# Attention and a gated MoE layer on one core: one pair's x transposed on TensorE, and the first MoE matmuls of three chunks in whole tiles

## The chip, the core and the metric

The kernel runs on one core of a Trainium2 chip. The metric is the device time of one execution in microseconds (us), a median over runs. The engines are named as in the profile: PE is TensorE (with PEld for its weight loads), ACT is ScalarE, DVE is VectorE, POOL is GpSimd, and SP is SyncE, which computes nothing here and only issues DMAs.

## The reference, cut to what matters

Batch B = 8, heads H = 8, tokens per batch S = 576, head size D = 64. Attention is causal with a window of 128 and a bias that falls with distance; its output, 4608 rows of 512, is the input x of a layer with 2048 hidden columns.

```python
scores = scale * np.matmul(q, k.transpose(0, 1, 3, 2))
bias = slopes[:, None, None] * (-np.abs(rel))[None, :, :]
mask = (rel >= 0) & (rel < window)
scores = np.where(mask, scores + bias[None], -1e9)
attn = softmax(scores)
out = np.matmul(attn, v)
x = out.transpose(0, 2, 1, 3).reshape(B * S, H * D)
h = x @ w_in
g = h * np.cos(h)
return g @ w_out
```

## The kernel before

**Units of attention.** A batch is split into nine units. Unit (pr, G) is head pair pr (0 to 3, two heads, 128 rows of x) and token group G: G = 0 is tokens 0 to 255 of the batch, G = 1 tokens 256 to 511. The ninth unit, the tail, is tokens 512 to 575 of all heads. A unit runs through PE (scores, L631, for the tail L621), ACT (exponential, L668), DVE (a multiplication with a stored bias mask, L686 to L693), PE (PV, the product with V, L725 and L728, for the tail L711 and L713), and DVE (division by the sum of the row, L765 and L767, into a buffer `xnat`). Units are run three at a time: (0,0), (1,0), (2,0); then (3,0), (0,1), (1,1); then (2,1), (3,1) and the tail. The three use PSUM bank pairs (2,3), (4,5), (6,7).

**x has to be transposed** into `xT` (head pair's 128 columns on the partitions, tokens along the free side) before it can enter the MoE layer. `x_back` does that, in one of two ways: batches 0 and 1 with two TensorE transposes into the unit's own PSUM bank (L800) and a copy by ACT or DVE (`flex`, L419 and L420); batches 2 to 7 with a DMA transpose that SP issues (L788; for the tail L780).

**MoE.** The 4608 tokens are cut into nine chunks of 512, which do not line up with batches of 576: chunk 2 is tokens 1024 to 1535, and batch 2 begins at token 1152. MoE1 makes h for a chunk: 16 column groups fc of 128, each a sum over the four head pairs kc. It has two forms. The whole form (`moe1`, L837) has four matmuls of 512 columns for one fc. The half form (`moe1_half`, L852) takes 256 tokens (hf = 0 or 1) and two column groups, and has eight matmuls of 256 columns. Either fills one PSUM bank of 512 columns, followed by a cosine on ACT (L823) and a multiplication on DVE (L829) into `gT`. MoE2 (L863) multiplies `gT` with w_out, 64 matmuls of 512 columns per chunk, copies the result to `ob` (L419, L420) and stores it by an SP DMA (L877).

**Rounds.** Round c does MoE1 of chunk c, and then attention of batch c + 1 with MoE2 of chunk c filling PE in between. Near its end MoE1 of chunk c + 1 begins as well. In chunks 1 to 3 all of MoE1 is in half form; in chunks 4 to 7 the first 8 of 16 column groups are in half form (all four fc pairs for hf 0, then for hf 1) and the other 8 whole; chunk 8 is whole. Chunk 0 has its own hand-written list.

What a chunk needs of the newest batch: chunk 2, hf 0 (tokens 1024 to 1279) reaches 128 tokens into batch 2, so it needs the G = 0 units of all four pairs; hf 1 (1280 to 1535) needs their G = 1 units too. Chunk 5 (2560 to 3071) reaches 192 tokens into batch 5, chunk 6 (3072 to 3583) 128 tokens into batch 6, chunk 7 (3584 to 4095) 64 tokens into batch 7; in each only hf 1 does.

**What sets the order.** Each operation is recorded with what it reads and writes, an estimated duration and a priority. A list scheduler (`Plan.schedule`) orders the operations of every engine but POOL, from estimates of its own, and `emit` writes one fixed sequence per engine with the semaphore waits that are needed. So each engine runs strictly in its written order, and an operation that waits holds up all behind it. DMA issues of SP stand in one queue: x transposes (L788, L780), the transposes of the next batch's q and k (L590) and the output stores (L877). POOL issues the loads of q, k (L454) and v (L463) in the order in which they are recorded; from batch 4 on they wait for an x transpose of an earlier batch.

Of the kernel before, what the change touches and what calls it, by code (L numbers as in the profile page):

```python
# [20 lines left out]
SPLIT = 4  # L21
# [89 lines left out]
class Plan:  # L111
# [16 lines left out]
    def op(self, eng, fn, r=(), w=(), dma=None, occ=100, lat=None, pri=5, mode=0, table=None,  # L128
           pk=None, after=(), behind=()):
        o = Op()  # L130
        o.seq = len(self.all)
        o.eng = (eng,) if isinstance(eng, str) else tuple(eng)
        o.fn, o.r, o.w, o.dma = fn, tuple(r), tuple(w), dma
        o.occ, o.lat, o.pri, o.mode, o.table = occ, occ if lat is None else lat, pri, mode, table
        o.pk, o.banks = pk, {k[1]: None for k in o.w if k[0] == "B"}
        preds = {d: ORDER for d in behind}
        preds.update((d, DATA) for d in after)
        for k in o.r:
            if k in self.writer:
                preds[self.writer[k]] = DATA  # L140
        for k in o.w:
            if k in self.writer:
                preds[self.writer[k]] = DATA
                if k[0] == "B":
                    o.banks[k[1]] = self.writer[k]
            for d in self.readers.get(k, ()):
                preds.setdefault(d, WAR)
        if dma is not None and dma in self.lastdma:
            preds[self.lastdma[dma]] = DATA
        if eng == "pool":  # L150
            if eng in self.lastseq:
                preds.setdefault(self.lastseq[eng], ORDER)
            self.lastseq[eng] = o
        if dma is not None:
            self.lastdma[dma] = o
        o.preds, o.succs, o.npred = preds, [], len(preds)
        for d in preds:
            d.succs.append(o)
        for k in o.r:
            self.readers.setdefault(k, []).append(o)  # L160
        for k in o.w:
            self.writer[k], self.readers[k] = o, []
        self.all.append(o)
        return o
# [199 lines left out]
def bass_alibi_sliding__then__act_gcu_kernel(  # L364
# [8 lines left out]
    with ExitStack() as ctx:  # L373
# [43 lines left out]
        def flex(o, i, w, n, pri, after=()):  # L417
            op(("act", "dve"),
               {"act": lambda e: e.activation(o, i, ACTF.Copy),  # L419
                "dve": lambda e: e.tensor_copy(o, i)},  # L420
               w=w, occ={"act": 95 + int(0.84 * n), "dve": 70 + int(1.05 * n)},
               lat={"act": 200 + int(0.84 * n), "dve": 140 + int(1.05 * n)}, pri=pri,
               after=after)
# [63 lines left out]
        def turn(kind):  # L487
            if phase[0] % 2 != kind:
                phase[0] += 1
                f = ACTF.Sin if kind else ACTF.Exp  # L490
                op("act", lambda e: e.activation(warm[:, :], halfpi[:, 0:1], f, scale=0.5),  # L491
                   r=["halfpi"], w=["warm"], occ=150, lat=230, table=phase[0], pri=0)
# [107 lines left out]
        def units(b):  # L600
            full = [(pr, G) for G in range(2) for pr in range(NPAIR)]
            return [(b, u) for u in full + [("t", None)]]
# [171 lines left out]
        def xkeys(pr, t0, n):  # L774
            return [("xT", pr, t // 64) for t in range(t0, t0 + n, 64)]

        def x_back(b, u, s, i):
            if u[0] == "t":
                t0 = S * b + 512
                o = op("sp", [lambda e: e.dma_start_transpose(xT[:, :, t0:t0 + 64], xtl[i][:, :])],  # L780
                   r=[("xtl", i)], w=[k_ for pr in range(NPAIR) for k_ in xkeys(pr, t0, 64)],
                   dma=f"xt{i}", occ=1250, pk=(256, 0.92, True), pri=2)
                xops.append(o)
                return
            pr, G = u
            t0 = S * b + 256 * G
            if b >= 2:
                o = op("sp", [lambda e: e.dma_start_transpose(  # L788
                    xT[:, pr, t0:t0 + 256].rearrange("p (r t) -> p r t", r=2), xnat[i][:, :])],
                   r=[("xnat", i)], w=xkeys(pr, t0, 256), dma=f"xb{i}", occ=1250,  # L790
                   pk=(256, 0.92, True), pri=2)
                xops.append(o)
                return
            bank = SLOT[s][0]
            dst = ps[:, bank, :].bitcast(BF16)[:, 768:1024]

            def f(e):
                ins = None
                for r in range(2):
                    ins = e.transpose(dst[:, 128 * r:128 * r + 128],  # L800
                                      xnat[i][:, 128 * r:128 * r + 128], ident[:, :])
                return ins
            op("pe", f, r=[("xnat", i), "ident"], w=[("B", bank)], occ=120, lat=290, pri=0)
            flex(xT[:, pr, t0:t0 + 256], dst, [("B", bank)] + xkeys(pr, t0, 256), 256, 0)
# [27 lines left out]
        def moe1(c, fc, bank):  # L832
            ci = ccount[0] % NCOS
            ccount[0] += 1
            gi = c % 2
            for kc in range(NPAIR):
                op("pe", lambda e, kc=kc: e.matmul(  # L837
                    ps[:, bank, :], w_in[:, kc, 128 * fc:128 * fc + 128],
                    xT[:, kc, CH * c:CH * c + CH], start=(kc == 0), stop=(kc == NPAIR - 1)),
                   r=xkeys(kc, CH * c, CH) + [("wi", fc)], w=[("B", bank)],  # L840
                   occ=216, lat=379, pri=5)
            gcu(c, bank, gT[gi][:, fc, :], [("g", gi, fc, 0), ("g", gi, fc, 1)], ci)

        def moe1_half(c, hf, f2, bank):
            ci = ccount[0] % NCOS
            ccount[0] += 1
            gi = c % 2
            t0 = CH * c + 256 * hf
            for i in range(2):
                fc = 2 * f2 + i  # L850
                for kc in range(NPAIR):
                    op("pe", lambda e, i=i, fc=fc, kc=kc: e.matmul(  # L852
                        ps[:, bank, 256 * i:256 * i + 256], w_in[:, kc, 128 * fc:128 * fc + 128],
                        xT[:, kc, t0:t0 + 256], start=(kc == 0), stop=(kc == NPAIR - 1)),
                       r=xkeys(kc, t0, 256) + [("wi", fc)], w=[("B", bank)],
                       occ=110, lat=271, pri=5)
            gcu(c, bank, gT[gi][:, 2 * f2:2 * f2 + 2, 256 * hf:256 * hf + 256],
                [("g", gi, 2 * f2 + i, hf) for i in range(2)], ci)
# [22 lines left out]
        def moe2(c):  # L881
            yield
            for t in range(4):
                cols = [(0, 512, OB[t % 2])] if c < NCH - 1 or t < 3 else [(0, 384, 1), (384, 128, 2)]
                for c0, wd, bank in cols:
                    moe2_mm(c, t, bank, c0, wd)
                    store(c, t, bank, c0, wd)
# [12 lines left out]
        def load_qk(b, after=()):  # L900
            for t in range(NBLK):
                load_nat("q", q, b, t, after)
                load_nat("k", k, b, t, after)
# [17 lines left out]
        for c in range(NCH):  # L921
            turn(1)
            if c:
                n = (0, 8, 8, 8, SPLIT, SPLIT, SPLIT, SPLIT, 0)[c]
                for i in range(2 * n):
                    moe1_half(c, i // n, i % n, 2 + i % 6)
                for i in range(16 - 2 * n):
                    moe1(c, 2 * n + i, 2 + (2 * n + i) % 6)
            second = moe2(c)
            if c + 1 < B:  # L930
                us = units(c + 1)
                if c == 0:
                    play(1, SECOND)
                else:
                    cross_transposes(c + 1)
                    if c == 1:
                        load_v(2, after=crossed[3:4])
                        load_qk(3)
                        load_v(3)
                    for g in range(0, 9, 3):  # L940
                        run(us[g:g + 3], (1, 2, 3))
            if c == 0:
                load_qk(2)
            else:
                if 3 < c + 2 < B:
                    load_v(c + 2, after=xops[3:4] if c > 2 else xops[-1:])
                if c + 3 < B:
                    load_qk(c + 3, xops[-1:])
            for _ in second:
                pass  # L950
# [29 lines left out]
```

## Time and profile before

| | us |
|---|---|
| median of 4 runs | 313.27 (312.67 to 314.71) |
| the profiled execution | 313.67 |
| its span in the profile | 311.6 |

The granted TensorE clock was 1.0 throughout. The groups around the change, from the table of the costliest groups (count, busy us, mean ns of one):

| group | count | busy | mean |
|---|---|---|---|
| L863 PE, MoE2, mostly 512 columns | 565 | 132.4 | 373 |
| L852 PE, MoE1 half form, 256 columns | 768 | 90.5 | 273 |
| L837 PE, MoE1 whole form, 512 columns | 186 | 41.5 | 379 |
| L800 PE, transposes of x | 32 | 4.5 | 221 |
| L419 ACT, copy of x after them, 128x256 | 8 | 3.0 | 380 |
| L823 ACT, cosine | 144 | 94.9 | 686 |
| L829 DVE, multiplication | 144 | 95.1 | 686 |
| L788 SP, x transposes by DMA | 48 | | 4.4 us to landing (2.3 to 8.6) |

A PE row's mean is the time of one matmul from start to its modelled end; matmuls overlap, so their pace is read from the chain of waits, which charges each only until the next one starts. Some records of matmuls are missing (565 of 576 for MoE2, 186 of 192 for the whole form). "Landing" is the time from a DMA's issue to its semaphore. The times in the views are from the span's start.

### The profile page before, as it was taken

What the parts mean: (1) busy time and instruction counts of PE and PEld (TensorE: products, weight loads), DVE (VectorE), ACT (ScalarE), POOL (GpSimd) and SP (SyncE); (2) the same over time, 40 slices, a digit from 0 to 9 for tenths busy, and PEclk for the clock granted to TensorE, in tenths of its full rate; (3) what the DMA queues carried; (4) which work ended last, traced back from release to release, by engine and by line L of the source; (5) the groups of instructions that cost most, each with busy time, mean ns of one, the idle gap of its engine ahead of it and who ended that gap; (6) DMA issues with size and microseconds to landing.
All of it is one profiled execution on the core that took longest, in us unless ns stands there. A gap on an engine that the chain in (4) does not pass through costs nothing.

```text
span 311.6 us, 6884 instructions
## 1 busy us (share of the span) xinstructions
PE 299.8 (96%) x2738; PEld 186.0 (60%) x2772; DVE 196.9 (63%) x445; ACT 204.6 (66%) x298; POOL 105.9 (34%) x134
## 2 busy tenths in 40 slices
PE   6799999999979999999999999999999999999996
PEld 4488555884558557855754485456645764444444
DVE  3898667786668767876787578755867684353000
ACT  8797846985567748874986488746784786462211
POOL 8999910049706400780356054605000000000000
PEclk9999999999999999999999999999999999999999
DMA  9999999969999982999999999999933300101112
GB/s 133 166 194 193 192 173 191 164 78 164 182 151 139 144 127 68 119 154 187 144 179 150 184 125 153 141 147 153 119 70 93 76 13 0 67 2 67 67 69 101
DMA packets 160895, 39.25 MB, mean 126 GB/s; under 512 B 148960, under 2 KB 156384, under 8 KB 160864
## 3 DMA queue, kind: packets, MB, share of 16 engines
q0 software_dynamic: 109552, 18.10, 80.3%
q1 hardware_dynamic: 51312, 20.72, 35.3%
q8 instruction: 22, 0.36, 0.5%
q14 instruction: 9, 0.07, 0.1%
HBM read 36.70 MB, written 9.44 MB: 148 GB/s over the span
## 4 chain that ended last, share of the span: by engine, by line
PE 82%; DMA 8%; POOL 7%; issue 2%; DVE 1%; ACT 0%; POOLq 0%
PE ps L863 37%; PE ps L852 22%; PE ps L837 13%; DMA vp<-in_v_dram 5%; PE ps L631 4%; DMA xT<-xnat 3%; PE ps L725 2%; POOL w_inb L470 2%; PE ps L728 1%; POOL vp L463 1%; POOL w_outb L477 1%; PE ps L711 1%; POOL qnat L427 1%; POOL knat L427 1%; PE ps L713 1%
## 5 line engine op out<-in xcount | busy, mean ns | idle before, releaser
L863 PE MATMUL ps<-w_outb,gT 128*128 128x512 bf16 (+2 forms) x565 | 132.4, 373 | 2.4 <-issue 1.6
L829 DVE TENSOR_TENSOR gT<-ps,cos 128x512 bf16<-128x512 f32 x144 | 95.1, 686 | 27.6 <-ACT cos L823 14.1
L823 ACT ACTIVATE cos<-ps,halfpi 128x512 f32<-128x512 f32 x144 | 94.9, 686 | 24.0 <-PE ps L852 10.0
L852 PE MATMUL ps<-xT,w_inb 128*128 128x256 bf16 x768 | 90.5, 273 | 1.9 <-DMA xT<-xnat 1.9
L863 PEld LDWEIGHTS ps<-w_outb,gT 128*128 128x128 bf16 x592 | 52.5, 98 | 52.6 <-issue 1.6
L852 PEld LDWEIGHTS ps<-xT,w_inb 128*128 128x128 bf16 x768 | 72.7, 98 | 12.3 <-DMA xT<-xnat 2.1
L668 ACT ACTIVATE p<-ps 128x768 bf16<-128x768 f32 (+1 forms) x64 | 54.8, 917 | 30.5 <-PE ps L631 15.3
L463 POOL DMA_DIRECT2D vp<-in_v_dram x40 | 34.7, 909 | 85.3 <-DMA xT<-xnat 37.1
L419 ACT ACTIVATE ob<-ps 128x512 f32<-128x512 f32 (+2 forms) x23 | 13.3, 580 | 43.3 <-PE ps L863 43.2
L837 PE MATMUL ps<-xT,w_inb 128*128 128x512 bf16 x186 | 41.5, 379 | 0.3
L454 POOL DMA_DIRECT2D qnat<-in_q_dram x32 | 29.6, 925 | 22.6 <-DMA xT<-xtail 22.6
L837 PEld LDWEIGHTS ps<-xT,w_inb 128*128 128x128 bf16 x192 | 18.8, 98 | 21.8 <-DVE gT L829 0.5
L454 POOL DMA_DIRECT2D knat<-in_k_dram x32 | 29.5, 923 | 0.4 <-issue 0.4
L767 DVE TENSOR_TENSOR xnat<-ps,rec 128x256 bf16<-128x256 f32 x64 | 26.7, 420 | 1.9
L686 DVE TENSOR_TENSOR p<-p,emask 128x1024 bf16<-128x1024 bf16 x32 | 21.8, 685 | 9.3 <-ACT p L668 9.1
L725 PEld LDWEIGHTS ps<-vp,p 128*128 128x128 bf16 x256 | 17.0, 97 | 14.1 <-issue 10.1
L691 DVE TENSOR_TENSOR p<-p,emask 128x256 bf16<-128x256 bf16 x32 | 9.0, 282 | 21.5 <-ACT p L668 21.1
L725 PE MATMUL ps<-vp,p 128*128 128x65 bf16 x256 | 21.9, 193 | 0.6 <-DVE p L686 0.4
L728 PE MATMUL ps<-vp,p 128*128 128x65 bf16 x192 | 20.0, 193 | 0.0
L491 ACT ACT_TABLE_LOAD x15 | 19.2, 1283 | 0.3
L631 PEld LDWEIGHTS ps<-qt,kt 64*128 64x128 bf16 x320 | 11.8, 94 | 11.5 <-issue 7.8
L631 PE MATMUL ps<-qt,kt 64*128 64x128 bf16 (+1 forms) x320 | 18.1, 238 | 0.3
(58 smaller groups left out, 168.0 us busy)
## 6 DMA issues: line engine op xcount, KB each, us to landing
out_dram<-ob SPq DMA_DIRECT2D x35, 256.0 KB, 4.0
vp<-in_v_dram POOLq DMA_DIRECT2D x32, 128.0 KB, 5.8
knat<-in_k_dram POOLq DMA_DIRECT2D x25, 128.0 KB, 7.2
qnat<-in_q_dram POOLq DMA_DIRECT2D x25, 128.0 KB, 7.0
w_inb<-in_moe_w_in_dram POOLq DMA_DIRECT2D x8, 256.0 KB, 8.4
w_outb<-in_moe_w_out_dram POOLq DMA_DIRECT2D x6, 256.0 KB, 13.9
qnat<-in_q_dram POOLq DMA_DIRECT2D x3, 256.0 KB, 10.0
knat<-in_k_dram POOLq DMA_DIRECT2D x3, 256.0 KB, 12.7
```

Source lines behind the costliest of these rows:

```text
L454: op("pool", [lambda e: e.dma_start(nat[w][b % 2][0:rows, t, :].rearrange("p (h d) -> p h d", h=H), src[b, :, 128 * t:128 * t + rows, :].r ...
L463: op("pool", [lambda e, t=t, rows=rows: e.dma_start(vp[b % 2][0:rows, t, :, 0:64], v[b, :, 128 * t:128 * t + rows, :].rearrange("h p d -> ...
L631: ins = e.matmul(ps[:, banks[x], c0:c1], keys_ap(i, x, pr, kc), query_ap(i, x, pr, qb, nb), start=True, stop=True)
L668: op("act", lambda e: e.activation(P[i][:, :, lo:512], src_[:, :, lo:512], ACTF.Exp, scale=0.125), w=held + [("P", i)], occ=920 if u[1] el ...
L725: ins = e.matmul(o, P[i][:, x, d0:d0 + 128], V[:, kc, h, 0:65], start=True, stop=not two)
L728: ins = e.matmul(o, P[i][:, x, p0:p0 + 128], V[:, kc - 1, h, 0:65], start=False, stop=True)
L767: op("dve", lambda e: e.tensor_tensor(o, U[:, :, :, 0:64], rv[:, :, :, None].broadcast_to([128, 2, 2, 64]), ALU.mult), r=[("rec", ri)], w= ...
L823: op("act", lambda e: e.activation(cosb[ci][:, :], h, ACTF.Sin, bias=halfpi[:, 0:1]), r=["halfpi"], w=[("B", bank), ("cos", ci)], occ=586, ...
L829: op("dve", lambda e: e.tensor_tensor(o, h, cs, ALU.mult), r=[("cos", ci)], w=[("B", bank)] + keys, occ=606, lat=692, pri=3)
L837: op("pe", lambda e, kc=kc: e.matmul(ps[:, bank, :], w_in[:, kc, 128 * fc:128 * fc + 128], xT[:, kc, CH * c:CH * c + CH], start=(kc == 0), ...
L852: op("pe", lambda e, i=i, fc=fc, kc=kc: e.matmul(ps[:, bank, 256 * i:256 * i + 256], w_in[:, kc, 128 * fc:128 * fc + 128], xT[:, kc, t0:t0 ...
L863: op("pe", lambda e, fc=fc: e.matmul(ps[:, bank, 0:wd], gT[gi][:, fc, 128 * t:128 * t + 128], w_out[:, fc, c0:c0 + wd], start=(fc == 0), s ...
```

## The change

In batch 2, unit (3,0), the last of the four pairs of the first token group, takes the TensorE way of `x_back`: two PE transposes and a copy take the place of one SP DMA transpose. And in chunks 5, 6 and 7 all 16 column groups of MoE1 are in whole form: `SPLIT` (4) becomes 0, so the first loop, over half-form tiles, is empty, and the second makes all 16.

```diff
@@ x_back
             pr, G = u
             t0 = S * b + 256 * G
-            if b >= 2:
+            if b > 2 or (b == 2 and u != (3, 0)):
                 o = op("sp", [lambda e: e.dma_start_transpose(
                     xT[:, pr, t0:t0 + 256].rearrange("p (r t) -> p r t", r=2), xnat[i][:, :])],
                    r=[("xnat", i)], w=xkeys(pr, t0, 256), dma=f"xb{i}", occ=1250,
@@ the loop over chunks
             if c:
-                n = (0, 8, 8, 8, SPLIT, SPLIT, SPLIT, SPLIT, 0)[c]
+                n = (0, 8, 8, 8, SPLIT, 0, 0, 0, 0)[c]
                 for i in range(2 * n):
                     moe1_half(c, i // n, i % n, 2 + i % 6)
                 for i in range(16 - 2 * n):
```

Since the scheduler makes the order anew, the fixed sequences of PE, DVE, ACT and SP differ from round 1 on; POOL's is the same.

## Prediction

> **What bounds the kernel now.** I read the page first: its busy table, then its chain of waits.
>
> ```profile
> span 311.6 us, 6884 instructions
> PE 299.8 (96%) x2738; PEld 186.0 (60%) x2772; DVE 196.9 (63%) x445; ACT 204.6 (66%) x298; POOL 105.9 (34%) x134
> PE 82%; DMA 8%; POOL 7%; issue 2%; DVE 1%; ACT 0%; POOLq 0%
> ```
>
> TensorE (PE) is busy 96% of the span; the other engines have a third or more of it free. So the time is PE's work plus PE's holes. The view of waits, cut to PE between 59 and 265 us, lists the holes:
>
> ```profile
> PE ps L852 <- DMA xT<-xnat: 1.9, 1, 1.9
> PE ps L863 <- issue: 1.4, 9, 0.2
> ```
>
> (Columns: total us, times, longest.) One hole of 1.9 us, and nine of 0.2. The chain of waits, in order of time, shows what the big one waits for, and the timeline what stands around it:
>
> ```profile
> 80.92 0.34 DVE xnat L767
> ...
> 81.28 8.57 DMA xT<-xnat
> 89.85 0.05 issue
> 89.90 0.28 PE ps L852
> ```
>
> ```profile
> 87.53 0.49 PE L852 MATMUL ps<-xT,w_inb 128*128 128x256 bf16 x3
> ...
> 89.90 0.28 PE L852 MATMUL ps<-xT,w_inb 128*128 128x256 bf16 x1 [1.87 <-DMA xT<-xnat]
> ```
>
> (First two numbers: start and length in us.) x of unit (3,0) of batch 2 is finished at 81.26; its transpose is issued by SP at 81.28 and lands at 89.85. The 4th matmul of MoE1's group (kc = 3, the last head pair) needs it. Matmuls of this line step by 0.109, so after starts at 87.53, 87.64 and 87.75 it was due at 87.86; it started at 89.90. The true hole is 2.04 us; the view says 1.87 because a matmul's modelled end lies behind its issue slot. PE issues in order, so the tail's 16 PV matmuls, ready in time, stand behind it.
>
> **The change, part 1: unit (3,0) of batch 2 through TensorE.** It removes one SP transpose and adds two 128x128 PE transposes into the unit's PSUM bank and one 128x256 copy. In the built order of the changed kernel they stand after the 8 PV matmuls of unit (0,1) and one MoE2 matmul. Those PV matmuls end at 81.28; one MoE2 step (0.216, below) later is 81.5, and xnat is ready at 81.26, so they do not wait. Their price on PE is read from pairs of batch 1 in the chain: 0.14 to 0.22 in these rows, and I take 0.16.
>
> ```profile
> 43.44 0.16 PE ps L800 x2
> 54.64 0.22 PE ps L800 x2
> 58.72 0.14 PE ps L800 x2
> ```
>
> The copy stands on ScalarE between two exponentials; the group's row gives 380 ns. ScalarE's exponentials of that run start at 78.14 and take 2.64 (to 80.78), the next starts at 84.11 after 3.33 idle: the copy costs nothing there. Without that cover it would delay one exponential by 0.38. xT is ready near 82.3, against 85.8, the new place of the first kc = 3 (85.31 + 0.16 + 3 x 0.109). The 2.04 us goes.
>
> [...]
>
> **What is late next.** With 2.04 us less, MoE1 of chunk 2 reaches its second half of tokens earlier, and that half needs x of all four G=1 units. SP's queue and the two single issues around 87 to 89 (time to landing, last number):
>
> ```profile
> 81.28 3.93 SPq L788 DMA_TRANSPOSE xT<-xnat  x3
> 85.31 0.52 SPq L877 DMA_DIRECT2D out_dram<-ob  x1
> 87.36 2.46 SPq L788 DMA_TRANSPOSE xT<-xnat  x2
> ```
>
> ```profile
> xT<-xnat SPq DMA_TRANSPOSE x1, 7.8
> xT<-xnat SPq DMA_TRANSPOSE x1, 6.9
> ```
>
> Pair 2 lands at 87.36 + 7.8 = 95.2, pair 3 at 88.57 + 6.9 = 95.5 (the second issue of that group starts at 88.57). The changed order here is 6 half-form matmuls, 8 PV, 6, 8 PV, 8, 16 PV, then 108: exactly what round 2 does already, where it takes from 118.76 to 122.00, 3.24 us. MoE1 starts at 85.31, plus 0.16 for the transposes: 85.47 + 3.24 = 88.7. The first half has 64 matmuls, 20 done; 44 more at 4.80 (the row below) end at 93.5. Pair 2 is wanted at 93.7, pair 3 at 93.8. If they land when they did, PE waits 95.5 - 93.8 = 1.7 us: the upper bound. The lower is 0, because the queue that carries them was behind by several us and has one 64 KB transpose less ahead: before, units landed 0.8 and 1.2 us apart there (81.28 + 8.6 = 89.9, 82.59 + 8.1 = 90.7, 83.92 + 7.9 = 91.8), and up to 89.3 the first one's own packets ran. Moving up by one place, 0.8 to 1.2, leaves 0.5 to 0.9 of the wait; moving up by the whole time in which (3,0) held the queue, about 3 us from 86 to 89, leaves none. I take 0.3, nearer to none, because the loads of V that contend there end at 93.4 in any case and PE's step into the half is not a hard edge.
>
> **Part 2: chunks 5 to 7 whole in 512 tokens.** Per chunk 64 matmuls of 256 columns become 32 of 512; three chunks: 192 become 96. Pace from the chain:
>
> ```profile
> 184.77 4.80 PE ps L852 x44
> 277.22 3.45 PE ps L837 x16
> ```
>
> 4.80/44 = 0.1091, 3.45/16 = 0.2156. Saving 96 x (2 x 0.1091 - 0.2156) = 0.25 us. 96 weight loads vanish, but each (98 ns) was already hidden under a matmul. ScalarE and VectorE still do 16 tiles of 128x512 per chunk, so cosine and multiply stay the same (686 ns each against 0.87 of PE per tile).
>
> [...]
>
> What it adds is a wait: a whole matmul of chunk 5, 6 or 7 reads x of the next batch's unit (pair,0) at once, where the first half-form ones read only older batches. Behind it on PE stand the PV matmuls of the round's last units. Before, (3,0) landed at 180.0, 210.7 and 244.3 (177.73 + 2.3, 208.45 + 2.3, 240.26 + 4.0), and kc = 3 would be due at 181.48 + 3 x 0.216 = 182.1; at 214.16 + 0.65 + 0.25 (8 PV stand between) = 215.1; and at 244.57 + 0.9 = 245.5. All have room, 1.2 us at least; queue and PE move together with the earlier start. Cost 0, upper bound (the longest landing seen, 8.6, in round 6) 240.26 + 8.6 - 245.5 = 3.4.
>
> The order elsewhere differs only in where MoE2 fills; sequence changes cost PE about 0.1 each and their number stays. The POOL queue's order is unchanged. Bounds of this reshuffling: -0.2 to +0.3, taken 0.
>
> **Sum.** -2.04 + 0.16 + 0.3 - 0.25 = -1.83. The profiled execution would go from a span of 311.6 to 309.8; it had 313.67 in all (2.07 around the span), 0.4 above the median of 313.27. Against the median: 311.4 us.
>
> **Rivals.**
> (A) As summed: 311.4; with the second wait from 0 to 0.6 and the reshuffling, 310.9 to 311.9.
> (B) The second wait takes the place of the first: pairs 2 and 3 land as late as before. -1.83 - 0.3 + 1.7 = -0.4: 312.8. For it: the landings of 6.9 and 7.8 us, with data in the queue's hands from 87.36 only, which is when xnat was ready. Against: the shorter queue.
> (C) Slower: in the changed order of SP in round 4, the last K transpose of batch 5 (64 rows) stands behind a store and three x transposes, where it was ahead of them. The tail's score matmuls (L621) need it. The store needs a copy that ended at 172.15, about 170.3 now; three issues at 1.25 to 2.7 us each put the K transpose at 174.5 to 176; landing takes 2.3 (same order, round 5: issued 206.87, landed 209.15) to 7.3 us (its own landing here before): 176.8 to 183.3. The scores were due at 179.67, minus 1.83, plus 7 MoE2 matmuls now ahead of them (1.5): 179.3. At worst PE waits 4.0: +2.2, 315.4. It turns the sign when the landing is later than 181.2. For it: 7.3 us here. Against: that latency came from POOL's loads of batch 6, the last of which landed at 176.88.
> (D) Whole matmuls wait in rounds 4 to 6, and give back about 1.5: 312.9. Against: the margins above.
>
> **How the numbers follow.** A 0.66, B 0.19, D 0.06, C 0.09. Half a per cent, about what a measurement of this kernel can tell from no change, is 1.57 us, so the line lies at 311.7, inside A's range: I leave 0.05 of A on the near side. Faster 0.61; same 0.30 (0.05 + B + D); slower 0.09. The predicted time is A's, 311.4. The range reaches to B and D and a little of the reshuffling above them, and 0.9 below A for the bounds that gain (no second wait, 0.3; reshuffling, 0.2; and 0.4, by which one run stood off the median): 310.5 to 313.2. A's own: 310.9 to 311.9.
>
> **What would show it.** Right: no wait of L852 on xT<-xnat near 88 us, a pair of L800 near 81.5, the wait list of PE between 59 and 265 us with nothing above 0.6, L852 576 times and L837 288 times, and the first half-form matmul of chunk 2's second half near 93.5. Wrong: a wait on xT<-xnat between 93 and 95.5 of more than 1 us (B), of L621 on kt<-knat near 180 (C), of L837 on xT<-xnat near 182, 215 or 245 (D).

## The result, and the profile after

The changed kernel's median is 312.53 us (54 runs), against 313.71 of the kernel before in its 78 runs: ratio 0.996, 95% interval 0.995 to 0.997. That is 1.2 us less, where 1.83 was forecast (311.4 against a median of 313.27, which more runs moved to 313.71). The time lies in the range, but outside A's own range of 310.9 to 311.9 (311.3 to 312.3, if it moves up with the median of before): the forecast's likeliest case was too good by a third. The change is also less than the half per cent at which the prediction drew its line, so that what came is its "same" (0.30) and not its "faster" (0.61). The profiled execution took a span of 310.9 us, against 311.6.

The page of the changed kernel, its busy table and the two MoE1 groups:

```profile
span 310.9 us, 6701 instructions
PE 300.9 (97%) x2642; PEld 177.4 (57%) x2678; DVE 195.6 (63%) x443; ACT 206.2 (66%) x301; POOL 105.7 (34%) x134
...
L852 PE MATMUL ps<-xT,w_inb 128*128 128x256 bf16 x576 | 67.5, 273 | 0.0
L837 PE MATMUL ps<-xT,w_inb 128*128 128x512 bf16 x279 | 64.0, 379 | 0.5
```

The half form went from 768 to 576 matmuls as forecast, the whole one to 288 (279 have records). Its view of waits for PE between 59 and 265 us has one line:

```profile
PE ps L863 <- issue: 0.5, 3, 0.2
```

The wait on `xT<-xnat` is gone in this execution. The chain in order of time shows the new transposes:

```profile
83.02 0.22 PE ps L863
83.24 0.11 PE ps L800 x2
83.35 0.05 issue
83.40 0.38 PE ps L863
```

They stand where the prediction put them, one MoE2 matmul after the PV of unit (0,1); they cost 0.11, or 0.16 with the issue time behind them, and wait for nothing. SP's queue:

```profile
77.28 3.81 SPq L788 DMA_TRANSPOSE xT<-xnat  x3
81.84 0.34 SPq L877 DMA_DIRECT2D out_dram<-ob  x1
83.98 2.46 SPq L788 DMA_TRANSPOSE xT<-xnat  x2
86.89 0.34 SPq L877 DMA_DIRECT2D out_dram<-ob  x1
88.97 2.46 SPq L788 DMA_TRANSPOSE xT<-xnat  x2
```

Everything here is 1.4 to 1.6 us later than in the first profile of before (its first group of transposes starts at 75.73), although PE's order up to the new transposes is the same. The first weight load for the tail's scores (L621) starts at 34.51 us in that profile and at 35.89 in this one. That head of the program varies by itself, as the next runs show, so spans are not compared below, but the time from that load to the end, which contains everything that changed: 277.10 us before, 275.01 after. This one pair says 2.1, more than the runs say. Either the pair is lucky, or something is lost that it does not show.

### The profile page after: what moved, and what is told of

It is laid out like the page before. It is cut to its first block, busy times and chain, and to the rows that moved or that the text cites. A ratio compares the mean times of both kernels' runs of the same rounds, so it can differ in the third digit from the quotient of the medians.

```text
span 310.9 us, 6701 instructions
## 1 busy us (share of the span) xinstructions
PE 300.9 (97%) x2642; PEld 177.4 (57%) x2678; DVE 195.6 (63%) x443; ACT 206.2 (66%) x301; POOL 105.7 (34%) x134
## 4 chain that ended last, share of the span: by engine, by line
PE 83%; POOL 8%; DMA 6%; issue 1%; ACT 0%; DVE 0%; POOLq 0%
PE ps L863 37%; PE ps L837 20%; PE ps L852 16%; DMA qnat<-in_q_dram 6%; PE ps L631 4%; PE ps L725 2%; POOL vp L463 2%; POOL w_inb L470 2%; PE ps L728 2%; POOL w_outb L477 1%; POOL knat L427 1%; PE ps L711 1%; POOL qnat L427 1%; PE ps L713 1%; PE ps L621 1%
## 5 line engine op out<-in xcount | busy, mean ns | idle before, releaser
L829 DVE TENSOR_TENSOR gT<-ps,cos 128x512 bf16<-128x512 f32 x144 | 94.8, 685 | 28.8 <-PE ps L863 15.0
L852 PE MATMUL ps<-xT,w_inb 128*128 128x256 bf16 x576 | 67.5, 273 | 0.0
L837 PE MATMUL ps<-xT,w_inb 128*128 128x512 bf16 x279 | 64.0, 379 | 0.5
L852 PEld LDWEIGHTS ps<-xT,w_inb 128*128 128x128 bf16 x576 | 54.5, 98 | 7.3 <-issue 0.5
L837 PEld LDWEIGHTS ps<-xT,w_inb 128*128 128x128 bf16 x288 | 27.3, 98 | 32.2 <-DVE xtail L756 1.1
L419 ACT ACTIVATE ob<-ps 128x512 f32<-128x512 f32 (+2 forms) x25 | 14.5, 582 | 43.9 <-PE ps L863 43.7
L631 PE MATMUL ps<-qt,kt 64*128 64x128 bf16 (+1 forms) x320 | 18.8, 246 | 0.2 <-ACT kt L419 0.2
```

Source lines behind the costliest of these rows:

```text
L631: ins = e.matmul(ps[:, banks[x], c0:c1], keys_ap(i, x, pr, kc), query_ap(i, x, pr, qb, nb), start=True, stop=True)
L829: op("dve", lambda e: e.tensor_tensor(o, h, cs, ALU.mult), r=[("cos", ci)], w=[("B", bank)] + keys, occ=606, lat=692, pri=3)
L837: op("pe", lambda e, kc=kc: e.matmul(ps[:, bank, :], w_in[:, kc, 128 * fc:128 * fc + 128], xT[:, kc, CH * c:CH * c + CH], start=(kc == 0), ...
L852: op("pe", lambda e, i=i, fc=fc, kc=kc: e.matmul(ps[:, bank, 256 * i:256 * i + 256], w_in[:, kc, 128 * fc:128 * fc + 128], xT[:, kc, t0:t0 ...
```

## The experiments

**The kernel before again.** No edit.

> The kernel before, unchanged, for a second profile. Time up to the first tail score matmul (34.5 us in the first profile of before, 35.9 in that of after, though the order up to there is the same): if the head of the program varies by itself, it lies elsewhere again, between 33.5 and 37. Theory A (the hole is a fixed cost): L852 waits 1.9 us on xT<-xnat near 88 us whatever the head took. Theory B (the loads run on their own clock, so a late head eats into the hole): wait and head add up to a constant; a head at 35.9 goes with a hole of some 0.5 to 1.

Measured: head 35.20; from there to the end 276.30. Its waits of PE between 59 and 265 us:

```profile
PE ps L852 <- DMA xT<-xnat: 1.1, 1, 1.1
```

By the starts of the matmuls (as 2.04 was read in the prediction) this is 1.24. So the hole is not the constant of Theory A. It shrank by 0.8 with a head that was 0.7 later, as in Theory B.

**The changed kernel again, beside its two parts.** No edit for the first.

> The changed kernel, unchanged, timed beside its parts. Ratio 0.994 to 0.997 (0.996 measured). From the first tail score matmul to the end the profile takes about 275.0 us as in the first profile of after, whatever its head took (Theory A: 1.8 to 2.3 less than before each time).

Part 1 alone:

```diff
-            if b >= 2:
+            if b > 2 or (b == 2 and u != (3, 0)):
```

> Part 1 alone: x of (3,0) of batch 2 on TensorE, chunks 5 to 7 as before. Prediction's sum: -2.04 + 0.16 + 0.3 = -1.6 us, ratio 0.995. Rival (part 1 gives all that was measured, part 2 nothing or less): 0.996, as the whole change. No wait on xT<-xnat near 88 us; second half of chunk 2 waits 0 to 0.3.

Part 2 alone:

```diff
-                n = (0, 8, 8, 8, SPLIT, SPLIT, SPLIT, SPLIT, 0)[c]
+                n = (0, 8, 8, 8, SPLIT, 0, 0, 0, 0)[c]
```

> Part 2 alone: MoE1 of chunks 5 to 7 whole, x of batch 2 as before. Prediction's sum: -0.25 us, ratio 0.999; rival: the whole form or the order it brings costs something, ratio 1.000 to 1.003, which would explain the 0.6 us missing. The wait of 1.9 us on xT<-xnat near 88 stays.

Measured: 0.9951 (0.9927 to 0.9975) for the whole change, 0.9998 (0.9969 to 1.0027) for part 1 alone, 0.9989 (0.9959 to 1.002) for part 2 alone. Part 1 alone gave no measurable gain, where 0.995 or 0.996 was expected, though its interval still reaches 0.9969. The timeline of PE in the second profile of the changed kernel tells where its gain goes:

```profile
86.56 0.38 PE L852 MATMUL ps<-xT,w_inb 128*128 128x256 bf16 x2
87.34 0.61 PE L852 MATMUL ps<-xT,w_inb 128*128 128x256 bf16 x4 [0.40 <-DMA xT<-xnat]
```

PE stops after two matmuls, kc = 0 and 1, not three: it is the third pair, unit (2,0), whose x is late now. By the starts this wait is 0.57 us. Part 1 alone has it too (0.91 us by the starts):

```profile
PE ps L852 <- DMA xT<-xnat: 0.7, 1, 0.7
```

And part 2 alone, where (3,0) still goes by DMA and PE's order up to here is that of before, waits for both units, (2,0) and then (3,0):

```profile
87.71 0.28 PE L852 MATMUL ps<-xT,w_inb 128*128 128x256 bf16 x1 [0.67 <-DMA xT<-xnat]
...
90.84 0.28 PE L852 MATMUL ps<-xT,w_inb 128*128 128x256 bf16 x1 [0.63 <-DMA xT<-xnat]
```

By the starts, 0.85 and 0.80. The wait on (2,0) therefore does not need the change; it comes and goes by execution.

The later rounds are compared from the first tail score of round 2 to the end. Here three profiles of before agree to 0.01 us (194.70 to 194.71), and so do three of after (195.34 to 195.37), but after has 5 MoE2 matmuls fewer done by then (164 weight loads against 169, at equal counts of everything else but the two new transposes), 5 x 0.2158 = 1.08 us. So after is 195.36 - 1.08 - 194.70 = 0.42 us shorter there. Part 2 alone takes 194.29, 0.41 shorter, with the same 169 done. Part 1 alone takes 196.29 with 164 done, 0.5 longer than before. Part of this is a stop near the end, which the chain of part 1 alone shows:

```profile
262.79 8.00 PE ps L863 x37
270.79 0.01 issue
270.80 0.70 DVE gT L829
271.50 0.04 issue
271.55 5.35 PE ps L837 x24
```

After 40 MoE2 matmuls (37 recorded) whole tiles of chunk 8 wait for VectorE, 0.29 us by the starts; the first profile of the changed kernel has no such stop there. The order made for part 1 alone costs 0.5 in rounds 3 to 8, and with part 2 beside it that cost is not there. Where the other 0.2 of it lies is open.

**x of (2,0) on TensorE as well.**

```diff
-            if b > 2 or (b == 2 and u != (3, 0)):
+            if b > 2 or (b == 2 and u not in ((2, 0), (3, 0))):
```

> The changed kernel with x of (2,0) of batch 2 on TensorE too. Theory B (the transposes land on the loads' clock; once (3,0) is gone the next one out, (2,0), is waited for: 0, 0.4 and 0.7 us by the profiles so far): no wait on xT<-xnat between 59 and 100 us whatever the head took, two more PE transposes for 0.16, so 0.2 to 0.4 us less than the changed kernel on average, ratio 0.994 to 0.9955. Rival (the missing 0.6 us went elsewhere, in rounds 2 to 8): no gain, ratio 0.996 to 0.997.

Measured: 0.9959 (0.9943 to 0.9976). PE has no listed wait at all between 59 and 265 us, at a head of 34.43 us, the earliest but one of all profiles. So the mechanism holds in this one profile. The time does not show it: 275.38 from the first tail score, where three profiles of the changed kernel have 275.01, 275.47 and 276.16 (below). On the mean that is 0.17 less, which the interval cannot tell: 0.9959 lies between the two forecasts. The order was made anew again: up to the tail score of round 2 the time is 0.34 less than the changed kernel's mean, and behind it 0.17 more (194.88 with 167 MoE2 weight loads done, against 195.36 with 164).

**The loads of V of batch 3 later.** Two runs, on the kernel before and on the changed one:

```diff
                         load_qk(3)
-                        load_v(3)
@@
+                if c == 1:
+                    load_v(3, after=xops[-1:])
                 if c + 3 < B:
                     load_qk(c + 3, xops[-1:])
```

> The kernel before, with nothing on TensorE and no whole chunks, but the five loads of V of batch 3 after the tail's x transpose of batch 2 instead of ahead of its first units. If contention with POOL's loads is what makes the landing take 7 to 9 us, (3,0) lands within 5 us of its issue near 82 to 83, before 88, and L852 does not wait near 88: ratio 0.995 to 0.997. If SP's queue or the transposes themselves are slow, it still lands near 89.8 and the wait of 1 to 2 us stays: ratio 1.000. The loads now contend in round 2, where a new wait may appear.

> The changed kernel with the same later loads. If contention is the cause, the wait on (2,0) is 0 in each execution: 0.2 to 0.5 us less than the changed kernel, ratio 0.994 to 0.9955; if not, 0.996.

Measured: 1.0054 (1.0033 to 1.0074) and 1.0001 (0.9977 to 1.0025), where the changed kernel has 0.996: both lose, against what was expected of contention. The chain of the first run names two landings:

```profile
81.17 5.98 DMA xT<-xnat
...
111.58 7.29 DMA xT<-xnat
```

Without the V loads beside it, (3,0) lands 6.0 us after its issue, where the other six profiles with it on DMA have 7.5 to 8.6; the two units behind it land after 5.0 and 3.9 us, against 7.3 to 8.9 in the three profiles of before. In round 2, where the loads went, the first three transposes land after 7.3, 6.8 and 7.3 us, against 2.3 to 4.7. So contention with POOL's V loads is part of the landing time there, for (3,0) some 2 us, if the new order is not part of it too. But the scheduler, with the loads gone from its own estimates, put the use of (3,0) earlier as well: PE was there at 85.5 and waited 1.67 us by the starts. And in round 2 a second wait of 1.58 appeared.

On the changed kernel the waits are 1.05, and in round 2 0.32 and 1.19. The first of them is for (2,0):

```profile
79.51 7.96 DMA xT<-xnat
```

The V loads are gone, and it still lands no sooner than in the changed kernel itself (6.9 to 8.3 us, below). They are not what makes (2,0) late.

**The kernel before, a third time.** No edit.

> The kernel before, a third profile, for head against hole. Theory B: hole = 2.04 us at a head of 34.51 and 1.24 at 35.20 (start to start), falling about 1 us for each us of head, so about 36.55 - head, not below 0.3. Theory A: between 1.9 and 2.1.

Measured: head 35.07, hole 1.01 by the starts, where Theory B said 1.5 and Theory A about 2. Neither fits. From the first tail score to the end, 276.06.

**Extra work ahead of the hole.** If a late PE eats into the hole, extra PE work ahead of it is partly free.

```diff
-                    op("pe", lambda e, i=i, fc=fc, kc=kc: e.matmul(
+                    op("pe", lambda e, i=i, fc=fc, kc=kc: (i + kc or (c, hf, f2) != (1, 1, 0) or [e.matmul(
+                        ps[:, bank, :], zero[:, 0:128], zero[:, :], start=True, stop=True)
+                        for _ in range(6)]) and e.matmul(
```

> The kernel before with 6 extra 512-column matmuls on zeros (6 x 0.216 = 1.3 us of PE, overwritten at once, no other order changed) in the middle of MoE1 of chunk 1, behind the head and ahead of batch 2's transposes. Theory B (the transposes land on the loads' clock, the hole takes up lateness of PE): the wait near 89 to 90 us shrinks by about what is added, from 1.0 to 2.0 down to 0 to 0.8, and the time grows by 0.2 to 0.5 us only: ratio 1.0005 to 1.002. Theory A (the hole is a fixed cost after the issue): wait 1 to 2 us still, 1.3 us more, ratio 1.004.

> The changed kernel with the same 6 extra matmuls. Both theories: it has next to no hole left to take them up, so 1.0 to 1.3 us more than the changed kernel: ratio to before 0.999 to 1.0. Theory B says that with the extra work the change is worth less than without it, 0.3 to 0.8 us against 1.2; Theory A that it is worth the same 1.2.

Measured: 1.0047 (1.0027 to 1.0067) and 0.9993 (0.9974 to 1.0011). The 1.3 us cost the kernel before 1.5 (0.8 to 2.1): nothing was absorbed, and Theory B falls. With the extra work in both kernels the change is worth 0.54%, 1.7 us, where Theory B had 0.3 to 0.8. The waits of the kernel before near 88 and 92 us, from the timeline, are as long as ever, 0.49 and 1.21 by the starts:

```profile
88.54 0.28 PE L854 MATMUL ps<-xT,w_inb 128*128 128x256 bf16 x1 [0.33 <-DMA xT<-xnat]
...
92.09 0.28 PE L854 MATMUL ps<-xT,w_inb 128*128 128x256 bf16 x1 [1.05 <-DMA xT<-xnat]
```

(L854 is L852 in this file.) Its transpose was issued at 83.81, 2.5 us later than in the first profile, and landed 8.24 us later all the same. That gave Theory C: PE's written order holds a fixed amount of work between the issue of (3,0)'s transpose and its use, 87.86 - 81.28 = 6.58 us, and the wait is the time to landing less that. With 8.57, 7.77 and 7.54 to landing in the three profiles of before it gives 1.99, 1.19 and 0.96; they waited 2.04, 1.24 and 1.01. In this run 8.24 gives 1.66 against 1.70 for both waits, and in part 2 alone 8.38 gives 1.80 against 1.65.

**The changed kernel, a third time.** No edit.

> The changed kernel, a third profile: the wait on xT<-xnat of (2,0) near 87 us is 0 to 0.7 us, less with a later head (0 at a head of 35.89, 0.57 at 35.58, start to start), and from the first tail score matmul to the end 275.0 to 275.7, against 276.1 to 277.1 in the three profiles of before.

Measured: 276.16 from the first tail score, head 35.01, and this wait, 1.38 by the starts:

```profile
PE ps L852 <- DMA xT<-xnat: 1.2, 1, 1.2
```

with, in the chain, the landing that ends it, of the transpose of (2,0):

```profile
79.17 8.26 DMA xT<-xnat
```

It is far outside the forecast of 0 to 0.7. The unit's three times to landing in the changed kernel, 6.87, 7.80 and 8.26, go with waits of 0, 0.57 and 1.38. It is the same rule with another unit, but counted from another point: (2,0) is third in its group, and its own issue slips with SP's queue. From the issue of the first of the three transposes to the use of (2,0), PE's order holds 9.87 us in each of the three profiles; (2,0) landed 9.42, 10.39 and 11.20 us after that issue, which gives 0, 0.52 and 1.33.

**Extra work between issue and use.** The same six matmuls on the kernel before, at `(c, hf, f2) != (2, 0, 1)`: just ahead of the first half-form matmul of chunk 2.

> The kernel before with the same 6 extra matmuls (1.3 us of PE, no other order changed), now between the issue of (3,0)'s transpose and its use: just ahead of the first half-form matmul of chunk 2. Theory C (formed from the five profiles in which (3,0) goes by DMA: wait = time to landing, 7.5 to 8.6 us, less the 6.5 us of work that PE's order has between issue and use): with 1.3 more between, the wait falls to 0 to 0.8, and the time grows by 0 to 0.4: ratio 1.000 to 1.0015. Rival (the landing comes a fixed time after PE's own progress, or the waits are not what costs): 1.3 us more as in the run with the extra work ahead, ratio 1.004 to 1.005.

Measured: 1.001 (0.9983 to 1.0038), and PE has no wait on `xT<-xnat` left. The timeline of PE (in this file the first row is the extra work, and L854 is again L852):

```profile
86.38 1.46 PE L852 MATMUL ps<-zero 128*128 128x512 bf16 x6
87.67 0.49 PE L854 MATMUL ps<-xT,w_inb 128*128 128x256 bf16 x3
88.68 0.49 PE L854 MATMUL ps<-xT,w_inb 128*128 128x256 bf16 x3
89.89 0.60 PE L854 MATMUL ps<-xT,w_inb 128*128 128x256 bf16 x4
```

The transpose was issued at 82.35 and took 7.8 us, so it landed near 90.1; kc = 3 is the last of the four matmuls, due at 89.89 + 3 x 0.109 = 90.2. The same 1.3 us of work that cost 1.5 us ahead of the issue costs about 0.3 behind it, and this was forecast from the rule. The two intervals overlap (from 1.0027 to 1.0038), and the wait is missing in a single profile, so the time and the profile support each other, and neither decides alone.

## Why the prediction was right or wrong

**What bounds the kernel:** right. PE is busy 97 or 98% of the changed kernel's three profiles, with at most one listed hole on a transpose's landing.

**"The 2.04 us goes":** the mechanism was right and its size was not. The hole for (3,0) is gone in every profile with part 1. But it was read from a single execution, and that was the largest of three: 2.04, 1.24, 1.01, on the mean 1.43. The term was 0.6 too large, by the luck of which execution was profiled.

**"What is late next":** the failed step, in its place and its size. It looked ahead, to the G = 1 units at 93.7 us, and took 0.3. Those were on time: in the changed kernel's first profile the second half was due near 95, and the two landed at 91.3 and 93.7; in its third, the closest, they landed at 94.6 and 94.8, due at 95.3 and 95.5. The next late one stood ahead of (3,0) in the same queue: unit (2,0), the third of the first group. In the first profile of before, SP's first group, the landing of its third transpose (issued at 78.31) and the first matmuls of chunk 2 are:

```profile
75.73 3.83 SPq L788 DMA_TRANSPOSE xT<-xnat  x3
```

```profile
xT<-xnat SPq DMA_TRANSPOSE x1, 6.7
```

```profile
85.31 0.49 PE L852 MATMUL ps<-xT,w_inb 128*128 128x256 bf16 x3
```

So it landed near 85.0 us (78.31 + 6.7), and the third of these matmuls used it at 85.5: 0.5 us of room. I had asked only when the unit in the removed wait would be ready. In the three profiles of the changed kernel it made waits of 0, 0.57 and 1.38, mean 0.65. Rival B's idea, a wait in place of the one removed, was right with another unit. The net gain of the waits is 1.43 - 0.65 = 0.78, where the sum had 2.04 - 0.3 = 1.74. Three profiles a side are few for waits that spread this much. With the parts alone and the two runs with extra work ahead of the issue, whose order around these waits is that of before or of the changed kernel, it is five a side: 2.04, 1.24, 1.01, 1.65 and 1.70 against 0, 0.57, 1.38, 0.91 and 0.09, a gain of 0.94.

**The transposes' price**, 0.16: confirmed, 0.11 to 0.16. Their copy stayed hidden: in the changed kernel's first profile ScalarE took 0.38 us for it at 83.38, and its next exponential waited for the tail's scores until 85.73.

**Part 2**, -0.25: the sign was right, and the size somewhat low: -0.41 alone, from the rounds after 2. The pace of the two forms accounts for 0.25; the other 0.16 must lie in the order made anew, which no run shows by itself.

**The reshuffling**, taken at 0 with bounds of -0.2 to +0.3: no fixed price. Part 1 alone lost 0.5 by it, outside these bounds, and with part 2 beside it that loss is not there.

**Waits of whole tiles (D) and of the last K transpose (C):** not there. (3,0) landed at 177.6, 209.6 and 239.6, before its use; the K transpose that was moved behind three x transposes was issued at 172.44, landed 4.3 us later at 176.7, and its scores began at 179.3.

**The sum, redone** from the first tail score to the end, three profiles against three: waits -0.78, transposes +0.13, later rounds -0.42, together -1.07. The profiles give 276.49 - 275.55 = 0.94 less, and the runs 1.2 (0.3 to 0.5% of 313.7, 0.9 to 1.6). The first pair of profiles, with 2.1, was the most favourable pairing of the nine. With so few profiles the close agreement is in part luck; the runs' interval is the firmer number.

**What stays open:** why a transpose takes 7.5 us to land in one execution and 8.6 in another. With the V loads away (3,0) landed about 2 us sooner and (2,0) did not; what makes one execution differ from the next was not tried. And no version clearly beat the changed kernel: with (2,0) on TensorE too, the waits are gone, but its time cannot be told from the changed kernel's.

## What to carry to other kernels

Here a wait on a DMA was its time to landing less the work that the waiting engine's own order holds between issue and use; 1.3 us of work put into that stretch cost about 0.3, and ahead of it 1.5. Where the issue itself queues, count from the issue that starts the queue. Before a wait is priced as a gain, list the room of every transfer that the same consumer needs, those ahead of the removed one in its queue first. And take the size of a wait on a DMA from several executions: here it was 1.0 to 2.0 us in the same program, as large a spread as the whole gain.

## What the runs showed of the hardware

In 4 of the 14 profiles, whose mean granted clock is 0.995 where the other ten have 0.999 or 1.00, the head of the program runs for one stretch of 3.4 us at half clock. In the changed kernel's first profile, the windows view has, per stretch, its length, the busy time of each engine (PE, PEld, DVE, ACT, POOL), then the granted clock (PEclk), and two columns on DMA:

```profile
11.00:14.50 3.50, 2.00 (x42) 1.26 (x39) 2.48 (x10) 2.08 (x5) 3.50 (x6) 1.00 1.82 163
14.50:17.90 3.40, 3.32 (x39) 1.85 (x40) 2.54 (x9) 3.08 (x5) 3.40 (x6) 0.50 1.49 193
17.90:21.00 3.10, 3.10 (x54) 2.88 (x52) 3.03 (x10) 3.07 (x6) 3.10 (x5) 1.00 1.46 196
```

PE had been busy for 2.0 of the 3.5 us ahead of it, with one wait of 1.2 us on `knat`. Part 1 alone has a stretch of 3.4 us at 0.50 as well, from 15.0 us, after 4.0 us in which PE was busy for 2.2. The first profile of before, with PE busy for 2.7 of the same 3.5 us and no wait longer than 0.5 in these windows, has clock 1.00 throughout. The waits near 88 us, of up to 1.9 us in the view of waits, brought no such stretch. What brings it on was not shown.

The stretch is likely one reason why the head varies between executions: the four profiles with it have heads of 35.6 to 36.0, the ten without it 34.4 to 35.6. It does not come from the change: the last run on the kernel before has it too (mean clock 0.995), and the order there is the same in all of them.
